# Second MLP layer as seven products of quarters, with the sums of the weight's quarters streamed from DRAM

## The chip, the cores and the metric

The kernel runs on one core of one Trainium2 chip. The metric is the device time of one execution in microseconds, the median of three runs. Instructions go to five engines, each with its own queue in program order: PE (matmul), DVE, ACT and POOL (elementwise work) and SP, which here only issues DMA transfers.

## The reference

Attention that keeps the 32 largest scores of each row, then a block with a Fourier mix and a two-layer MLP. All is float32; q, k and v are (8 batches, 8 heads, 576 tokens, 64), the weights 512x2048 and 2048x512.

```python
scores = q @ k.T / sqrt(64)
kth = np.partition(scores, -32, axis=-1)[..., -32:-31]
attn = softmax(np.where(scores >= kth, scores, -1e9))
x = (attn @ v)                       # heads joined: (8, 576, 512)
u = x + np.real(np.fft.fft(np.fft.fft(x, axis=1), axis=2))
un = (u - mean(u)) / np.sqrt(var(u) + 1e-6)     # over the 512 channels
out = u + np.maximum(un @ w_ch1, 0.0) @ w_ch2
```

## The kernel before

One loop counts steps `i`. A step is one 128-token tile of one head (or the 64 left-over tokens of two heads), 9 steps for a pair of heads, 36 for a batch (`PER_BATCH`), 288 for all (`N`). In a step PE computes scores for three steps ahead (`scores`) and ACT copies them from PSUM; DVE finds the 32 largest values by alternating MAX8 and MATCH_REPLACE8 (`top_ops`); ACT and POOL make the mask (`mask`), ACT the exponential (`expo`), and PE transposes the result two steps later (`transposes`) and multiplies it with v (`attend`).

Beside it goes the rest of a batch that has its attention behind it. POOL folds x into sums and differences (`fold_ops`), PE makes the DFT over the tokens (`dft_tokens`, tiles `yp`) and over the channels (`dft_channels`, tiles `mp`), adds the result to x and transposes it (`channels_first`, tiles `tpu`). Then the batch's MLP arrives as a queue of units (`mlp_units`). The five token tiles of a batch are two chunks: tiles 0, 1 and the 64 left-over tokens (320 columns), and tiles 2 and 3 (256 columns). For each chunk there are 16 units `hidden`, each of which makes 128 of the 2048 inner values, transposed, in PSUM tile `hp` and lets ACT write their ReLU to the SBUF tile `hT`; then units `back`: for a full tile 8 units of 2 products of 128x128 weights (a piece of hT) with 512 columns of w2, accumulated in one PSUM tile `cp`. The left-over tokens take 4 units, in which two halves of the inner sum go into two halves of the array. When a `cp` is done, ACT multiplies it by the row's 1/sqrt(var), POOL adds it to x, and SP stores x. For tile 3 DVE does both (`finish`), for the left-over tokens ACT and DVE.

The order of each engine is written by hand: `at(step, where, fn)` puts work at a step, `level` spreads the queued units evenly over the steps until the next batch's units arrive, and `some` lets units run between the fixed pieces of PE's work. w1, w2 and the tables stay in SBUF. SBUF tiles are named by `tag`, and tiles with one tag share a place: `hT` has one place, `S` (scores) six.

PSUM has eight banks of 512 float32 a partition: two for scores, two for transposes, one for the attention's product, and three (`ps_m`) for all that the MLP and the DFT make, and for a few other tiles, taken in turn.

The last batch has no attention beside it: after step 288 only its DFT and MLP (and the end of batch 6's MLP) are left.

Of the kernel before, what the change touches and what calls it, by code (L numbers as in the profile page):

```python
# [9 lines left out]
F32 = mybir.dt.float32  # L10
# [54 lines left out]
def kernel(  # L65
# [41 lines left out]
    batp = ctx.enter_context(tc.tile_pool(name="batp", bufs=1))  # L107
    small = ctx.enter_context(tc.tile_pool(name="small", bufs=4))
    ps_s = ctx.enter_context(tc.tile_pool(name="ps_s", bufs=2, space=bass.MemoryType.PSUM))
    ps_t = ctx.enter_context(tc.tile_pool(name="ps_t", bufs=2, space=bass.MemoryType.PSUM))  # L110
    ps_o = ctx.enter_context(tc.tile_pool(name="ps_o", bufs=1, space=bass.MemoryType.PSUM))
    ps_m = ctx.enter_context(tc.tile_pool(name="ps_m", bufs=3, space=bass.MemoryType.PSUM))

    ident = const.tile([P, P], F32, name="ident", tag="ident")
# [35 lines left out]
    def weight_steps(chunks, space, wc, slots):  # L150

        scaled = {}

        def words(n):
            o = 2 * wc * (n % slots)
            raw = space[:, o:o + 2 * wc]
            return raw, raw[:, 0:2 * wc:2], raw[:, 1:2 * wc:2]

        def load(n):
            if n < len(chunks):  # L160
                dst, src = chunks[n]
                if moe_w_ch1.dtype == F32:
                    nc.sync.dma_start(out=dst, in_=src)
                else:
                    nc.sync.dma_start(out=words(n)[0].bitcast(I32), in_=src.bitcast(I32))

        def scale_high(n):
            if moe_w_ch1.dtype == F32:
                return
            scaled[n] = ps_m.tile([P, wc], F32, name=f"wh_{n}", tag="mm")  # L170
            nc.scalar.activation(
                out=scaled[n], in_=words(n)[2], func=AF.Copy, scale=2.0 ** -112
            )

        def shift(n):
            if moe_w_ch1.dtype == F32:
                return
            nc.vector.tensor_scalar(
                out=chunks[n][0].bitcast(I32), in0=scaled.pop(n).bitcast(I32),
                scalar1=3, scalar2=None, op0=ALU.logical_shift_left,  # L180
            )

        def rest(n):
            if moe_w_ch1.dtype == F32:
                return
            _, low, high = words(n)
            nc.scalar.activation(
                out=low.bitcast(I32), in_=low.bitcast(U32), func=AF.Copy, scale=2.0 ** -29
            )
            nc.scalar.activation(out=high, in_=high.bitcast(I32), func=AF.Sign)  # L190

        def join(n):
            if moe_w_ch1.dtype == F32:
                return
            dst, (_, low, high) = chunks[n][0], words(n)
            bits = dst.bitcast(I32)
            nc.gpsimd.tensor_tensor(out=bits, in0=bits, in1=low.bitcast(I32), op=ALU.add)  # L197
            nc.gpsimd.tensor_tensor(out=dst, in0=dst, in1=high, op=ALU.mult)  # L198

        return load, scale_high, shift, rest, join  # L200


# [83 lines left out]
    def scores(i, part):  # L286
# [22 lines left out]
        if part == 1:  # L309

            pool, tag = (ps_s, "sp") if i else (ps_m, "mm")
            copy = nc.scalar.copy if i else nc.vector.tensor_copy
            sp = pool.tile([P, NF * P], F32, name=f"sp_{i}_t", tag=tag)

            q_end = P * t + rows
            nc.tensor.matmul(  # L316
                sp[:, 0:P], lhsT=qT[:, q_end - P:q_end], rhs=kt_t, start=True, stop=True
            )
            for h, (s_t, r, _, tails) in enumerate(to):
                copy(out=s_t[r, tails], in_=sp[P - rows:P, TAIL * h:TAIL * (h + 1)])  # L320
            return 0.3
# [156 lines left out]
    def to_tokens(pair, ch, at_once=True):  # L478
# [5 lines left out]
        xT, rd = xT_of.pop((pair, ch)), rd_of.pop((pair, ch))  # L484
        pool, tag = (ps_o, "o") if at_once else (ps_m, "mm")
        tp = pool.tile([P, 4, P], F32, name=f"tpx_{pair}_{ch}", tag=tag)
        for n, t in enumerate(CHUNKS[ch]):
# [104 lines left out]

    def dft_tokens(b, par):

# [3 lines left out]
        if b not in y_of:  # L598
            y_of[b] = batp.tile([P, 4, S], F32, name=f"y_{b}", tag="y")
        y = y_of[b]  # L600
        yps = [
            ps_m.tile([P, 2, KQ], F32, name=f"yp_{b}_{par}_{g2}", tag="mm") for g2 in range(2)
        ]

        def mm(g2, gg, st, lhsT, rows, table, start=False):

            nc.tensor.matmul(  # L607
                yps[g2][0:rows, gg, :],
                lhsT=lhsT,
# [6 lines left out]

        for g2 in range(2):
            for gg in range(2):
                g = 2 * g2 + gg
                for st in range(3):  # L620
                    f = fg[:, st] if st < 2 else ftail
                    mm(g2, gg, st, f[:, P * g:P * (g + 1)], P, gg, start=gg == 0 and st == 0)
        for st in range(3):
            mm(0, 1, st, zw[:, st, Q1:Q1 + 1] if st < 2 else ftail[:, DM:DM + 1], 1, 0)

# [3 lines left out]
        )  # L629
        for g2, yp in enumerate(yps):  # L630
            y2 = y[:, 2 * g2:2 * g2 + 2, :]
            nc.scalar.copy(out=y2[:, :, par:HS + 1:2], in_=yp[:, :, 0:KQ - par])
            nc.scalar.copy(out=y2[:, 0, mir], in_=yp[:, 0, back])
            nc.scalar.mul(out=y2[:, 1, mir], in_=yp[:, 1, back], mul=sg[:, g2:g2 + 1])
        if par == 1:
            tails_of_y(b)
        return 4.3

# [5 lines left out]
    def dft_channels(b, t, quick=False):  # L644

        rows, y = ROWS[t], y_of[b]
        mp = ps_m.tile([P, 2, DM // 2], F32, name=f"mp_{b}_{t}", tag="mm")
        for par in range(2):
# [61 lines left out]
    def channels_first(b, t):  # L710
# [3 lines left out]
        if (b, ch) not in unT_of:  # L714
            unT_of[b, ch] = batp.tile(
                [P, NDT, CW[0]], F32, name=f"unT_{b}_{ch}", tag="fold_s" if ch == 0 else "y"
            )
        tp = ps_m.tile([P, NDT, P], F32, name=f"tpu_{b}_{t}", tag="mm")
        for dt in range(NDT):
# [3 lines left out]
        nc.scalar.copy(out=unT_of[b, ch][:, :, col:col + rows], in_=tp[:, :, 0:rows])  # L723
        return 0.6

    def mlp_units(b):
# [4 lines left out]
        def hidden(ch, it):  # L733
            w, unT = CW[ch], unT_of[b, ch]
            if ch not in hTs:
# [3 lines left out]
                )  # L739
            hp = ps_m.tile([P, CW[0]], F32, name=f"hp_{b}_{ch}_{it}", tag="mm")  # L740
            for dt in range(NDT):
# [5 lines left out]

        cps, cts = {}, []

# [9 lines left out]
        def back(ch, t, part):  # L759
            n, hT, rs = CHUNKS[ch].index(t), hT_of[ch], rs_of[b]  # L760
            if part == 0:
                cps[t] = ps_m.tile([P, DM], F32, name=f"cp_{b}_{t}", tag="mm")
            cp = cps[t]
# [44 lines left out]
            if part == 3:  # L808
                ct = ct_of(t)
                for h in range(2):  # L810
                    r0 = TAIL + TH * h
                    nc.scalar.copy(out=ct[TH * h:TH * (h + 1), :], in_=cp[r0:r0 + TH, :])

                def finish():
                    xt, c = x[0:TAIL, 4, :], ct[0:TAIL]
                    nc.vector.tensor_tensor(out=c, in0=cp[0:TAIL], in1=c, op=ALU.add)
                    nc.vector.scalar_tensor_tensor(
                        out=xt, in0=c, scalar=rs[0:TAIL, 4:5], in1=xt, op0=ALU.mult, op1=ALU.add
                    )
                    for h in range(2):  # L820
                        tok = HS * h + 2 * P
                        nc.sync.dma_start(
                            out=out[b, tok:tok + TH, :], in_=x[TH * h:TH * (h + 1), 4, :]
                        )

                if last:
                    finish()
                else:
                    late_next.append(finish)

        units = []
        for ch in range(2):
            units += [
                (8 * CW[ch] / 1200.0, lambda ch=ch, it=it: hidden(ch, it), "hidden")
                for it in range(NIT)
            ]
            for t in CHUNKS[ch]:
                units += [
                    (1.75, lambda ch=ch, t=t, p=p: back(ch, t, p), "back")
                    for p in range(4 if t == 4 else 8)  # L840
                ]
        return units

# [97 lines left out]
    for c in range(DF // DM):  # L941
# [5 lines left out]
        )  # L947

    for b in range(B):
        end = PER_BATCH * (b + 1) - 1  # L950
# [39 lines left out]
        for par in range(2):  # L990
            at(ft[par], "pe1", lambda b=b, par=par: dft_tokens(b, par), 4.3)
        for n, t in enumerate((0, 1, 4, 2, 3)):
# [7 lines left out]
            if first and t == 4:  # L1000
                at(s + 1, "pe", lambda: (queue.extend(held), held.clear()) and 0.0)
        at(s + 1, "begin" if quick else "dve", lambda b=b: rsqrt(b))
        arrivals.append(s + (1 if quick else 2))
        at(arrivals[-1], "units", lambda b=b: (queue if b else held).extend(mlp_units(b)))

    queue, held, pending, written, now, out_next = [], [], [], set(), [0], []
    step_us = 6.0
# [13 lines left out]
    def level(i):  # L1021

        steps = range(i, next((a for a in arrivals if a > i), i + PER_BATCH))
        rest, lev = sum(u[0] for u in queue + held), 0.0
        while lev < 6.4 and sum(max(0.0, lev - fixed_cost(s)) for s in steps) < rest:
# [168 lines left out]
```

## Time and profile before

| | |
|---|---|
| median of three runs | 1944.0 us (1943.31 to 1945.73) |
| span of the profiled run | 1942.8 us |
| PE busy | 1831.8 us (94%) |
| DVE busy | 1577.0 us (81%) |
| ACT busy | 1205.3 us (62%) |
| POOL busy | 773.3 us (40%) |
| granted clock of PE, mean | 0.972 |
| DMA | 57.80 MB, mean 30 GB/s |

A busy share is a mean over the whole span. The page also divides the span into 40 slices, and there one sees which engine is full when. A group of instructions has a line, an engine, what it writes and reads, a count, its busy time and the mean length of one; the idle time after the bar is that of the engine just before them, with what ended it. PEld is PE's weight load.

### The profile page before, as it was taken

How to read it: one execution, taken by the hardware profiler on the slowest of the kernel's cores; microseconds unless marked ns; L12 is line 12 of the kernel's file. 1: busy time of each engine (PE TensorE's matmuls, PEld its weight loads, DVE VectorE, ACT ScalarE, POOL GpSimd, SP SyncE). 2: the span in 40 equal slices, each digit the busy share in tenths (PEclk: the TensorE clock that was granted, in tenths of full speed). 3: DMA queues.
4: the chain of work that ended last, by engine and by line, in shares of the span. 5: the costliest groups of instructions: out<-in, count | busy, mean ns of one | idle time of the engine just before them, and what ended most of it. 6: DMA issues, size and time to landing. Idle time of an engine off the chain costs nothing.

```text
span 1942.8 us, 27224 instructions
## 1 busy us (share of the span) xinstructions
PE 1831.8 (94%) x8624; PEld 1123.4 (58%) x8624; DVE 1577.0 (81%) x3245; ACT 1205.3 (62%) x3060; POOL 773.3 (40%) x1054
## 2 busy tenths in 40 slices
PE   6567799999999999999999999999999999998999
PEld 3344465564665656556664756556664756566655
DVE  8999989999999999888888879988888879843000
ACT  6878657776876667666666667666666757541100
POOL 4768642326523454235423444235523444222000
PEclk8877899999999999999999999999999999999999
DMA  5333000101001010010100110010000100000000
GB/s 164 105 90 106 19 13 19 33 19 30 19 19 33 19 30 13 13 33 19 30 19 19 27 24 21 11 33 19 24 19 24 27 24 19 1 14 1 11 14 11
DMA packets 133583, 57.80 MB, mean 30 GB/s; under 512 B 124352, under 2 KB 124480, under 8 KB 133440
## 3 DMA queue, kind: packets, MB, share of 16 engines
q1 hardware_dynamic: 132656, 55.85, 10.8%
q8 instruction: 69, 1.13, 0.2%
q14 instruction: 74, 0.61, 0.1%
q10 hardware_dynamic: 784, 0.21, 0.0%
HBM read 46.57 MB, written 9.44 MB: 29 GB/s over the span
## 4 chain that ended last, share of the span: by engine, by line
PE 79%; DVE 7%; POOL 7%; ACT 4%; issue 3%; DMA 0%; SPq 0%; POOLq 0%; DVEq 0%; ACTq 0%
PE hp L742 24%; PE cp L766 22%; PE o L448 7%; PE tpP L411 6%; PE sp L346 6%; PE yp L607 3%; DVE m L367 3%; PE cp L802 3%; DVE wk L369 2%; PE mp L656 2%; POOL wk L384 2%; PE sp_t L316 2%; POOL w L198 1%; POOL w L197 1%; PE tpk L260 1%
## 5 line engine op out<-in xcount | busy, mean ns | idle before, releaser
L384 POOL TENSOR_TENSOR wk<-S,wk 128x576 f32<-128x576 f32 x288 | 407.2, 1414 | 907.8 <-ACT wk L383 854.6
L367 DVE MAX8 m<-wk 128x8 f32<-128x576 f32 x864 | 623.7, 750 | 5.5
L742 PE MATMUL hp<-unT,w 128*128 128x256 f32 (+1 forms) x2048 | 539.0, 410 | 3.1 <-ACT unT L723 2.1
L766 PE MATMUL cp<-w,hT 128*128 128x512 f32 x1024 | 477.2, 598 | 0.0
L742 PEld LDWEIGHTS hp<-unT,w 128*128 128x128 f32 x2048 | 373.5, 191 | 126.2 <-issue 31.4
L369 DVE MATCH_REPLACE8 wk<-m,wk 128x576 f32<-128x576 f32 x576 | 427.7, 743 | 0.0
L766 PEld LDWEIGHTS cp<-w,hT 128*128 128x128 f32 x1024 | 179.4, 190 | 180.5 <-issue 179.9
L390 ACT ACTIVATE wk<-wk,nt 128x576 f32<-128x576 f32 x288 | 225.6, 783 | 54.3 <-POOL wk L384 53.4
L411 PE MATMUL tpP<-ident,wk 128*128 128x128 f32 x1152 | 185.4, 285 | 65.6 <-ACT wk L390 42.0
L414 ACT COPY PT<-tpP 128x512 f32<-128x512 f32 (+1 forms) x320 | 171.8, 549 | 119.1 <-PE tpP L411 116.5
L383 ACT ACTIVATE wk<-S,nt 128x576 f32<-128x576 f32 x288 | 227.7, 791 | 27.9 <-POOL nt L376 26.5
L411 PEld LDWEIGHTS tpP<-ident,wk 128*128 128x128 f32 x1152 | 140.9, 145 | 162.9 <-ACT wk L390 60.9
L746 ACT ACTIVATE hT<-hp 128x320 f32<-128x320 f32 (+1 forms) x256 | 105.1, 411 | 193.3 <-PE hp L742 191.0
L367 DVE MAX8 m<-S 128x8 f32<-128x576 f32 x288 | 214.0, 743 | 12.2 <-ACT S L320 11.9
L369 DVE MATCH_REPLACE8 wk<-m,S 128x576 f32<-128x576 f32 x288 | 213.8, 742 | 0.0
L448 PE MATMUL o<-PT,v 128*64 128x256 f32 (+3 forms) x1440 | 196.0, 416 | 2.1 <-ACT PT L414 1.6
L349 ACT COPY S<-sp 128x512 f32<-128x512 f32 (+1 forms) x264 | 142.2, 590 | 65.9 <-PE sp L346 65.6
L346 PE MATMUL sp<-kT,qT 64*128 64x512 f32 (+1 forms) x528 | 162.1, 675 | 4.3 <-ACT means L934 3.3
L448 PEld LDWEIGHTS o<-PT,v 128*64 128x64 f32 x1440 | 111.7, 153 | 75.7 <-issue 17.5
L780 DVE SCALAR_TENSOR_TENSOR x<-cp,gi,x 128x512 f32<-128x512 f32 x11 | 8.2, 746 | 128.3 <-PE cp L766 128.3
L316 PEld LDWEIGHTS sp_t<-kt,qT 128*128 128x128 f32 x320 | 56.4, 197 | 53.8 <-issue 20.0
L346 PEld LDWEIGHTS sp<-kT,qT 64*128 64x128 f32 (+1 forms) x528 | 43.0, 193 | 62.8 <-issue 44.5
(126 smaller groups left out, 1822.6 us busy)
## 6 DMA issues: line engine op xcount, KB each, us to landing
space<-in_moe_w_ch_dram SPq DMA_DIRECT2D x32, 512.0 KB, 3.6
nat<-in_q_dram SPq DMA_DIRECT2D x128, 64.0 KB, 2.1
v<-in_v_dram SPq DMA_DIRECT2D x128, 64.0 KB, 2.1
out_dram<-x SPq DMA_DIRECT2D x32, 256.0 KB, 2.1
nat<-in_k_dram SPq DMA_DIRECT2D x124, 64.0 KB, 2.1
nat<-in_q_dram SPq DMA_DIRECT2D x128, 8.0 KB, 1.7
v<-in_v_dram SPq DMA_DIRECT2D x128, 8.0 KB, 1.7
nat<-in_k_dram SPq DMA_DIRECT2D x124, 8.0 KB, 1.7
```

Of the source, the lines that this page charges most:

```text
L346: nc.tensor.matmul(sp[r], lhsT=qT[hd, q_cols], rhs=kT[hd, :], start=True, stop=True)
L349: nc.scalar.copy(out=s_t[r, keys], in_=sp[r])
L367: ops.append(lambda src=src, m8=m8: nc.vector.max(out=m8, in_=src))
L369: ops.append(lambda src=src, m8=m8: nc.vector.match_replace(w, m8, src, NEG))
L383: nc.scalar.activation(out=w, in_=Ssb[i], func=AF.Relu, scale=-FAR, bias=Nt[i][:, 1:2])
L384: nc.gpsimd.tensor_tensor(out=w, in0=Ssb.pop(i), in1=w, op=ALU.subtract)
L390: nc.scalar.activation(out=w, in_=w, func=AF.Exp, bias=Nt.pop(i)[:, 0:1], accum_out=den_t[pair % 3][:, c:c + 1],)
L411: nc.tensor.transpose(tp[:, c, :], p_sb[:, k0 + P * c:k0 + P * (c + 1)], ident)
L414: nc.scalar.copy(out=pt[:, NF * he:NF * (he + 1), col:col + w], in_=tp[:, :, o:o + w])
L448: nc.tensor.matmul(o[D * e:D * (e + 1), c0:c1], lhsT=vv[:, c, e, :], rhs=pt[:, 2 * NF if c == NF else NF * e + c, c0:c1], start=(c == 0), ...
L742: nc.tensor.matmul(hp[:, 0:w], lhsT=w1[:, dt, P * it:P * (it + 1)], rhs=unT[:, dt, 0:w], start=(dt == 0), stop=(dt == NDT - 1),)
L766: nc.tensor.matmul(cp, lhsT=hT[:, it, P * n:P * (n + 1)], rhs=w2[:, it, :], start=(it == 0), stop=(it == NIT - 1),)
```

## The change

A chunk's two full tiles times w2 is a product of a 2x2 block matrix (two token tiles, two halves of the inner 2048) with a 2x2 block matrix (two halves of the inner 2048, two halves of the 512 columns). The ordinary way needs eight products of quarters. Winograd's form of Strassen's scheme needs seven, with sums of quarters on both sides:

```text
S1 = A21 + A22   S2 = S1 - A11   S3 = A22 - S2   S4 = A12 - S2
T1 = B12 - B11   T2 = B22 - T1   T3 = B22 - B12  T4 = B21 - T2
P1 = A11 B11  P2 = A12 B21  P3 = S4 B22  P4 = A22 T4
P5 = S1 T1    P6 = S2 T2    P7 = S3 T3
U2 = P1 + P6   U3 = U2 + P7
C11 = P1 + P2   C12 = P5 + P3 + U2   C21 = P4 + U3   C22 = P5 + U3
```

Its purpose is to give PE an eighth less to multiply in the second layer. Batch 0 stays as it was. For batches 1 to 7:

- POOL makes T1 to T4 once, during batch 1's attention (`parts_of_w2`, 4 subtractions for each of 8 pieces), and SP writes them with B21 to a tensor in DRAM (`scr`, five parts of 8 pieces of 128x256).
- The places of w2's quarters B12 and B21 in SBUF (16 pieces) become a ring. `stream` lists the pieces in the order of their use; `take` hands the next one to a product, and once that is issued its place is refilled from DRAM by SP (`refill`), which waits for the product. B11 and B22 stay. After the last attention step six tiles of tag `S` add 12 places (`more_places`).
- POOL makes S1 to S4 in place in hT (`mix`, one operation on 8 pieces of 128x128 each).
- A product has 8 matmuls of 128x128 weights with 256 columns, in two units of four. P1, P2, P5 and P3 go through the two halves of PSUM tile X (`cx`), P4, P6 and P7 through Y (`cy`); the order is P1, P4, P2, P5, P6, P7, P3.
- ACT multiplies a result and POOL adds it to x, in pieces of 256 columns (`summed`); DVE makes U2 and U3 (`both`), and ACT and POOL bring them to x (`spread`). In the last batch DVE does all of it.
- X and Y live long, so the three banks of `ps_m` are now handed out by `bank`, which skips those that are held. `dft_tokens` is cut into two calls for each parity, with one tile each.
- The left-over tokens use B11 and B22, and then T1 and B21 from the stream (`tails`), with 256 columns a matmul.

The core of the diff:

```diff
+    def bank(shape, name, hold=False):
+        while turn[0] in held:
+            turn[0] = (turn[0] + 1) % 3
+        n = turn[0]
+        turn[0] = (n + 1) % 3
+        t = ps_m.tile(shape, F32, name=name, tag=f"m{n}", bufs=1)
...
-        yps = [
-            ps_m.tile([P, 2, KQ], F32, name=f"yp_{b}_{par}_{g2}", tag="mm") for g2 in range(2)
-        ]
+        yp = bank([P, 2, KQ], f"yp_{b}_{par}_{g2}")
...
+    for _ in range(B - 1):
+        for ch in range(2):
+            stream += [(o, kc) for o in (T4, B21, T1, T2, T3) for kc in range(NK)]
+            if ch == 0:
+                stream += [(o, kc) for kc in range(NK) for o in (T1, B21)]
...
+    def refill():
+        while places and coming:
+            n, (o, kc) = coming.pop(0)
+            loaded[n] = places.pop(0)
+            nc.sync.dma_start(out=loaded[n], in_=scr[:, o, kc, :])
...
+            def product(dst, a, of, part, start=False):
+                for kc in range(NK // 2 * part, NK // 2 * (part + 1)):
+                    rhs, done = of(kc)
+                    nc.tensor.matmul(
+                        dst, lhsT=h()[a][:, kc, :], rhs=rhs, start=start and kc == 0,
+                        stop=kc == NK - 1, skip_group_check=True,
+                    )
+                    done()
...
+            def mix(dst, a, c, op=ALU.subtract):
+                v = h()
+                nc.gpsimd.tensor_tensor(out=v[dst], in0=v[a], in1=v[c], op=op)
...
+            def p2(part):
+                product(got["X"][:, 0, :], "12", streamed(B21), part)
+                if part:
+                    summed(ta, lo, got["X"][:, 0, :], 3)
+                    mix("12", "12", "11")
+
+            def p5(part):
+                product(got["X"][:, 1, :], "21", streamed(T1), part)
+                if part:
+                    summed(tb, hi, got["X"][:, 1, :], 2)
...
+            units = [
+                (1.75, lambda f=f, part=part: f(part), "back")
+                for f in (p1, p4, p2, p5, p6, p7, p3) for part in range(2)
+            ]
...
+            if b:
+                units += fast(ch)
+                continue
...
+    for kc in range(NK):
+        at(PER_BATCH + 14 + 2 * kc, "pool", lambda kc=kc: parts_of_w2(kc))
+    at(PER_BATCH + 14, "load2", lambda: nc.sync.dma_start(out=scr[:, B21], in_=w2[:, NK:, 0:DH]))
+
+    at(N + 4, "load", more_places)
...
         for par in range(2):
-            at(ft[par], "pe1", lambda b=b, par=par: dft_tokens(b, par), 4.3)
+            for g2 in range(2):
+                at(ft[par], "pe1", lambda b=b, par=par, g2=g2: dft_tokens(b, par, g2), 2.15)
```

## The prediction

> **What bounds the kernel now.** I read the page's busy slices first, then the groups kept apart by shape, the timeline of PE, the windows and the waits. The slices say where an engine is full:
>
> ```profile
> PE   6567799999999999999999999999999999998999
> DVE  8999989999999999888888879988888879843000
> PEclk8877899999999999999999999999999999999999
> ```
>
> A slice is 48.6 us. DVE fills the first five (batch 0's attention, PE half idle). From slice 6 on PE is full to the end, at the full clock; after slice 36 there is no attention left and only PE works. The second layer of batches 1 to 7 lies from about 510 us on, all inside PE's full stretch. Between 800 and 1700 us the view of waits for PE lists five entries, 4.8 us in all. So there, time taken off PE's own work is time off the end, and a new wait of PE is time on it. What the concerned groups cost:
>
> ```profile
> L766 PE MATMUL cp<-w,hT 128*128 128x512 f32 x1024 | 477.2, 598 | 0.0
> L742 PE MATMUL hp<-unT,w 128*128 128x256 f32 x1024 | 240.3, 382 | 0.0
> L802 PE MATMUL cp<-w,hT 128*64 128x512 f32 x256 | 61.1, 603 | 0.0
> ```
>
> L766 has 8 x 64 = 512 products but 1024 records: each f32 product is two records. The mean is a latency; matmuls overlap, so the price is the spacing of starts in a long run:
>
> ```profile
> 1716.68 3.65 PE L802 MATMUL cp<-w,hT 128*64 128x512 f32 x16
> 1720.27 0.66 PE L411 MATMUL tpP<-ident,wk 128*128 128x128 f32 x4
> ...
> 1735.46 7.07 PE L742 MATMUL hp<-unT,w 128*128 128x256 f32 x32
> 1742.37 0.60 PE L411 MATMUL tpP<-ident,wk 128*128 128x128 f32 x4
> ...
> 1749.92 2.38 PE L448 MATMUL o<-PT,v 128*64 128x256 f32 x20
> 1752.23 3.72 PE L742 MATMUL hp<-unT,w 128*128 128x256 f32 x16
> ...
> 1802.37 12.18 PE L766 MATMUL cp<-w,hT 128*128 128x512 f32 x28
> 1814.39 16.05 PE L742 MATMUL hp<-unT,w 128*128 128x320 f32 x59
> ```
>
> First column start, second length. 28 records of 512 columns take 12.02 us: 429 ns each. 32 of 256 columns (a new weight load for each) take 6.91 us: 216 ns. So the price is proportional to columns, and halving the columns exposes no weight load. 64-row products of 512 columns: 3.59/16 = 224 ns; of 256 columns: 2.31/20 = 116 ns.
>
> **What the skill says.** (1) "TensorE: Matmul & The Clock Gate", Step-by-step: the next weights load while the present matmul streams. The trace agrees: loads are recorded at 190 ns, and 216 ns spacing holds. (2) "PSUM — Partial Sum Buffer", PSUM bank collisions: two engines may not touch one bank at a time, even at different columns, so order is kept by bank. Before, a tile has a bank to itself in this pool and nothing shows this; after, two products share a held bank. (3) "DMA: Bandwidth & Descriptors", Latency: some 2 us of fixed cost for a transfer. The DMA part of the page agrees, 2.1 us for 64 KB and 256 KB. (4) "GPSIMD Engine Reference", Specifications: SBUF interfaces shared with VectorE, with contention only for some DVE forms. MAX8 has 743 and 750 ns means whatever POOL does, so I charge nothing.
>
> **The change part by part.**
>
> Removed, for each of seven batches: 64 products of 512 columns, 64 x 2 x 0.429 = 54.9 us of PE. Added: 2 chunks x 7 products x 8 = 112 of 256 columns, 112 x 2 x 0.216 = 48.4. Saved 6.5 us a batch, 45.8 in all. The 64-token tail goes from 32 records of 224 ns to 64 of 116: +0.2 a batch, +1.5 in all. Net PE work: −44.3 us.
>
> The stream: 96 blocks of 128 KB a batch, 672 in all, refilled as a product has consumed its place. 16 places are four units of PE (1.7 us each) ahead, and units share PE with attention, so a refill has about 10 us; 28 places after attention. A transfer takes about 2.1 us to land. The queue's price of an issue is 0.48 us:
>
> ```profile
> 14.80 1.92 SPq L214 DMA_DIRECT2D nat<-in_q_dram  x4
> ```
>
> so 46 us more SP time per batch of some 215, where it now has about 50. A refill waits on SP for PE, and behind it stand the loads of q, k and v, needed four steps (24 us) later: free. In batch 7 PE eats a block in 0.43 us and SP refills in 0.48, but 28 are in hand for 40: free. DMA is under a tenth busy now. A wait on a landed transfer costs PE nothing visible: the five transposes of k with DMA waits at 826.82 us go in 0.54 us, as fast each as tpP's four in 0.43.
>
> POOL gains, per batch, 8 sums of 128x1024 (2.36 us, row L580), 8 adds of 256 columns (about 0.72, L549's 256-column row), two of 1.27 and two of 0.72, less three of 1.27: +25 us, from 87 to 112 of 215. Behind each stands the mask (L384) of the next tile, but
>
> ```profile
> POOL wk L384 <- ACT wk L383: 483.8, 128, 8.7
> ```
>
> says that in 800 to 1700 us POOL stood 484 us waiting for ACT before it, 3.8 us a time; a sum of 2.4 us goes there. ACT +4 us and DVE +1.2 us a batch are beside PE's work too. The 32 subtractions that make w2's sums (23 us of POOL, steps 50 to 64) lie in a POOL that is 30% busy; I charge 1 us.
>
> New waits of PE, from the instruction orders of both programs:
>
> (a) Two of the three banks of this pool are held by a chunk's X and Y. For batches 2 to 6 one pair of DFT tiles (yp) then shares the one bank that is left, with no unit between, so PE waits for ACT's three copies:
>
> ```profile
> 939.72 0.43 ACT L632 COPY y<-yp 128x288 f32<-128x288 f32 x1 [4.28 <-PE yp L607]
> 940.03 0.29 ACT L633 COPY y<-yp 128x144 f32<-128x144 f32 x1
> 940.20 0.41 ACT L634 ACTIVATE y<-yp,sg 128x144 f32<-128x144 f32 x1
> 940.47 0.43 ACT L632 COPY y<-yp 128x288 f32<-128x288 f32 x1
> ```
>
> 0.75 us, plus a drain of 0.16 (0.41 long, 0.25 spacing) and 0.2 of hand-over: 1.1 x 5 = 5.5 us.
>
> (b) In batches 3, 5 and 6 mp_0 and mp_1 share a bank too. Here ACT is late:
>
> ```profile
> 941.37 3.72 PE L656 MATMUL mp<-fd,y 128*128 128x256 f32 x16
> 944.74 1.17 ACT L673 COPY us<-mp 128x512 f32<-128x512 f32 x2
> ```
>
> mp_0's eight records end at 943.2, its copy at 945.3, as exp, score copies and a mask lie before it on ACT: 2.2 us x 3 = 6.6.
>
> (c) p5 writes the bank that ACT reads for p2 (the skill's point 2). Mostly other work of PE or a free ACT hides it; three chunks have only 0.43 us of transposes between, three of the last two batches nothing: 3 x 0.3 + 3 x 0.65 = 2.8.
>
> (d) Before batch 7's layer all fourteen tiles go through one bank, where ACT or DVE (0.6 to 0.7 us, plus 0.2) must empty each; units stand between some. About 0.4 + 4 x 0.85 + 3 x 0.75 = 6.0. Before, the same place has waits of 0.96 and 0.35, left as they are.
>
> (e) Batch 1's layer lies at 510 to 740 us, where DVE is nearly full as well:
>
> ```profile
> 631.41:680.00 48.59, 48.59 (x251) 33.53 (x250) 46.17 (x96) 33.89 (x88) 23.86 (x35) 1.00 0.09 19
> 825.69:874.30 48.61, 48.61 (x243) 28.19 (x242) 41.12 (x84) 31.30 (x80) 17.26 (x27) 1.00 0.13 33
> ```
>
> (Columns: PE, PE's loads, DVE, ACT, POOL.) At 631 DVE is 95% busy, at 826 85%. I count half of that batch's 6.5: −3.3 of gain.
>
> Sum: −44.3 + 5.5 + 6.6 + 2.8 + 6.0 + 3.3 + 1.0 = −19.1: **1925 us**. The doubtful prices are (a) to (d), 20.9 us: none if ACT is prompt and PE's waits displace others (1904), twice that if ACT is later than in the trace (1946).
>
> **The rivals.**
>
> Clean gain: the waits a to d mostly vanish, because a PE that has less work waits where it would have waited anyway, or ACT is prompt. For it: PE is the only full engine after 780 us. Against it: PE's order is fixed and these pairs stand back to back. 1925 less 20.9: about 1904 us.
>
> DVE or the chain over POOL takes over: DVE is needed 190 us of a batch's 215, in some stretches 95%; POOL's sums wait for PE in order, and mask, exp and transposes come behind. If half of the gain of batches 1 to 6 goes so (39 us x 1/2, less e) on top of the waits: 1925 + 16 = 1941. Against it: POOL's 3.8 us of slack and exp's place, 6 us after the mask.
>
> The stream starves PE, the side of slower: SP works strictly in order; stores that wait for POOL or DVE and blocks of 8 loads (8 x 0.48 = 3.8 us) stand between refills. If each of 14 chunks lost 3.8 us: 1925 + 53 = 1978. Against it: four units of lead.
>
> **How the numbers follow.** Forecast 0.52, clean 0.22, DVE or POOL 0.16, starved 0.10. The range 1902 to 1942 leaves out the starved case and the ends of the others. Faster: forecast, clean, and two thirds of the third case, 0.84; same (1940 to 1948) 0.05; slower: the starved case and the worst of the rest, 0.11.
>
> **What would show it.** Right: products of 256 columns at 216 ns spacing, no DMA among PE's waits, PE waits at yp, mp and tpu released by ACT or DVE of about 20 us, POOL near 960 us busy. Wrong: spacing above 230 ns in the streamed products (then weights or waits are exposed), DMA waits of PE, tpP waiting for exp, or DVE above 95% in every batch.

## The result

The changed kernel is slower: 1968.07 us (1964.51 to 1970.73, four runs) against 1944.76 us for the kernel before (four runs of its own). The ratio is 1.0119, with a 95% interval of 1.0098 to 1.0141. The profiled run has a span of 1964.0 us, 21.2 more than before.

### The profile page after: what moved, and what is told of

Read it like the earlier page. It is cut to its first block, busy times and chain, and to the rows that moved or that the text cites. A ratio compares the mean times of both kernels' runs of the same rounds, so it can differ in the third digit from the quotient of the medians.

```text
span 1964.0 us, 30502 instructions
## 1 busy us (share of the span) xinstructions
PE 1806.4 (92%) x9520; PEld 1275.7 (65%) x9520; DVE 1591.4 (81%) x3284; ACT 1225.0 (62%) x3128; POOL 961.6 (49%) x1196
## 4 chain that ended last, share of the span: by engine, by line
PE 69%; POOL 15%; ACT 6%; issue 5%; DVE 5%; DMA 0%; SPq 0%; POOLq 0%; DVEq 0%; ACTq 0%
PE hp L820 23%; PE cx L941 7%; PE o L465 7%; PE cy L941 6%; PE sp L363 5%; PE tpP L428 5%; POOL wk L401 4%; PE yp L622 3%; PE cp L1064 3%; PE mp L670 3%; POOL hT L960 2%; PE cp L844 2%; DVE m L384 2%; POOL w L215 2%; POOL w L214 2%
## 5 line engine op out<-in xcount | busy, mean ns | idle before, releaser
L401 POOL TENSOR_TENSOR wk<-S,wk 128x576 f32<-128x576 f32 x288 | 408.2, 1417 | 753.4 <-ACT wk L400 725.3
L400 ACT ACTIVATE wk<-S,nt 128x576 f32<-128x576 f32 x288 | 226.8, 788 | 94.4 <-POOL nt L393 93.4
L407 ACT ACTIVATE wk<-wk,nt 128x576 f32<-128x576 f32 x288 | 224.6, 780 | 75.6 <-POOL wk L401 74.2
L941 PE MATMUL cx<-w,hT 128*128 128x256 f32 x848 | 205.0, 388 | 10.0 <-issue 10.0
L941 PEld LDWEIGHTS cx<-w,hT 128*128 128x128 f32 x848 | 157.8, 194 | 39.7 <-issue 20.4
L960 POOL TENSOR_TENSOR hT<-hT 128x1024 f32<-128x1024 f32 x56 | 132.3, 2363 | 102.6 <-ACT hT L824 95.4
L941 PE MATMUL cy<-w,hT 128*128 128x256 f32 x648 | 156.2, 387 | 0.0
L941 PEld LDWEIGHTS cy<-w,hT 128*128 128x128 f32 x648 | 120.1, 193 | 24.6 <-issue 8.9
```

The lines of the kernel that those rows point to most:

```text
L400: nc.scalar.activation(out=w, in_=Ssb[i], func=AF.Relu, scale=-FAR, bias=Nt[i][:, 1:2])
L401: nc.gpsimd.tensor_tensor(out=w, in0=Ssb.pop(i), in1=w, op=ALU.subtract)
L407: nc.scalar.activation(out=w, in_=w, func=AF.Exp, bias=Nt.pop(i)[:, 0:1], accum_out=den_t[pair % 3][:, c:c + 1],)
L941: nc.tensor.matmul(dst, lhsT=h()[a][:, kc, :], rhs=rhs, start=start and kc == 0, stop=kc == NK - 1, skip_group_check=True,)
L960: nc.gpsimd.tensor_tensor(out=v[dst], in0=v[a], in1=v[c], op=op)
```

## The profile after

The page first: the totals, the slices that were shown of before and, as the last line, the chain that ended last, by engine:

```profile
PE 1806.4 (92%) x9520; PEld 1275.7 (65%) x9520; DVE 1591.4 (81%) x3284; ACT 1225.0 (62%) x3128; POOL 961.6 (49%) x1196
PE   6666799998999999999999999999999999998899
DVE  8999989998999979987888969897889878852110
PEclk8777899999999999999999999999999999999999
PE 69%; POOL 15%; ACT 6%; issue 5%; DVE 5%; DMA 0%; SPq 0%; POOLq 0%; DVEq 0%; ACTq 0%
```

The slices still look full, since a digit 9 hides up to a tenth. The sums tell more: PE is busy 25.4 us less than before, not 44, and idle 157.6 us (1964.0 − 1806.4) against 111.0. In the chain POOL has 15%, where it had 7% before:

```profile
PE 79%; DVE 7%; POOL 7%; ACT 4%; issue 3%; DMA 0%; SPq 0%; POOLq 0%; DVEq 0%; ACTq 0%
```

A window over most of the second layer shows the same. Columns: stretch, its length, then busy time (and instructions) of PE, PE's loads, DVE, ACT and POOL, the granted clock, DMA share and GB/s. Before:

```profile
480.00:1760.00 1280.00, 1268.70 (x6159) 780.55 (x6155) 1109.01 (x2293) 837.35 (x2136) 512.59 (x735) 1.00 0.09 21
```

After:

```profile
480.00:1760.00 1280.00, 1229.48 (x6762) 887.33 (x6759) 1110.33 (x2309) 847.65 (x2179) 638.05 (x814) 0.99 0.28 78
```

PE was idle 11.3 us of 1280, and is now idle 50.5. What it waits for is scattered, so I looked for the wait inside the attention loop that had grown most. It is one of ACT: in the view of waits over the whole run (time, number, longest) ACT's mask activation (L383 before, L400 after) waits for the bounds `nt` that POOL makes from the tile's largest and 32nd largest value. Before, then after:

```profile
ACT wk L383 <- POOL nt L376: 26.5, 21, 3.8
ACT wk L400 <- POOL nt L393: 93.4, 52, 4.9
```

One place in full, from the chain of waits (start, length, what; `issue` is time for which the profile shows no releaser):

```profile
915.98 0.73 POOL x L956
916.71 2.33 POOL hT L960
919.04 2.47 POOL zw L566 x2
921.51 0.16 POOL nt L393
921.67 0.02 issue
921.70 0.78 ACT wk L400
922.48 0.07 issue
922.55 1.41 POOL wk L401
923.96 1.35 issue
925.30 5.09 PE cx L941 x16
```

POOL works without a gap from 915.98: an addition to x, a sum of hidden blocks (L960), two folds of the DFT, and only then the bounds, which take 0.16 us. ACT stands at L400 until then, and behind it in ACT's queue are the exponential (L407), which also waits for POOL's subtraction L401, and the scaling (L955) that reads P2's result out of PSUM tile X. P5 goes into the other half of the same bank, so PE goes on with `cx` only when ACT has read it. ACT's and PE's timelines (start, length, what, and in brackets the idle time before; the last line is a place where PE has not waited):

```profile
921.70 0.77 ACT L400 ACTIVATE wk<-S,nt 128x576 f32<-128x576 f32 x1 [3.81 <-POOL nt L393]
923.98 0.78 ACT L407 ACTIVATE wk<-wk,nt 128x576 f32<-128x576 f32 x1 [1.04 <-POOL wk L401]
924.75 0.45 ACT L955 ACTIVATE hT<-cx,gi 128x256 f32<-128x256 f32 x1
921.61 0.49 PE L333 MATMUL sp_t<-kt,qT 128*128 128x128 f32 x2
925.30 5.09 PE L941 MATMUL cx<-w,hT 128*128 128x256 f32 x16 [3.21 <-issue]
711.85 3.62 PE L941 MATMUL cy<-w,hT 128*128 128x256 f32 x16
```

The reader is to see two losses: 3.21 us of waiting, and 16 records that take 5.09 us instead of 3.62. PE's granted clock is recorded as half for 3.41 us from 924.72 us on. The trace's clock records have seven such stretches between 500 and 1760 us; the trace of before has none there.

## The experiments

In all of them the kernel before was run beside the others on the same chip, 1942 to 1946 us. Ratios are to it, with their 95% interval. "Sums" are POOL's eight operations L960 a batch. The expectations call PE TensorE, DVE VectorE, ACT ScalarE and POOL GpSimd.

**Are the sums the cause?** The sums are left out (`mix` returns at once), so the output isn't the layer's.

```diff
             def mix(dst, a, c, op=ALU.subtract):
-                v = h()
-                nc.gpsimd.tensor_tensor(out=v[dst], in0=v[a], in1=v[c], op=op)
+                return
```

> After with the eight sums of hidden blocks per batch (L960, 56 of 2.36 us) left out, so the products multiply the plain blocks and the output is not the layer's; products, stream, banks, scaling and adds stay. Theory A (GpSimd's sums stand in its queue before the bounds of the next tile, L393; ScalarE's mask activation L400 waits for those, its copies out of PSUM come behind, TensorE waits and then runs at half clock): the loss goes, 1925 us (1915 to 1935), and ScalarE's wait at L400 falls from 93 us to about the 27 of before. Rival B (shared and held PSUM banks), rival C (stream) and rival D (256-column products cost more than their share): no change, 1962 to 1970.

Measured: 1929.42 us, 0.9927 (0.9912 to 0.9942). The sums cost 38.7 us, more than the whole loss. The rest of the change gains 14.8 us, not far from the 19 forecast. PE's busy time:

```profile
PE 1785.5 (93%) x9520; PEld 1264.4 (66%) x9520; DVE 1588.3 (82%) x3284; ACT 1225.7 (64%) x3128; POOL 830.9 (43%) x1140
```

The saving of PE is 46.3 us (1831.8 − 1785.5). The spans of the two profiled runs differ by 35.8 us, and the loss lies beside attention: its last transposes start at 1769.4 us with the sums and at 1734.6 without. Ahead of the changed layer, up to 480 us, PE is busy 4.8 us longer with the sums, which costs nothing, since the stretch is as long in both. From 480 us on, PE is busy 16.1 us longer for the same work and idle 19.7 us longer. The idle time is nearly all in three waits up to the end of attention: at `cx` 9.4 us (no wait shown there without the sums), at the transposes `tpP` for the exponential 10.3 (3.8), at `yp` for ACT's copies 8.6 (5.0). L400's wait fell from 93 to 42 us, where 27 was expected.

**By which way do they cost?** First the sums were put behind the bounds of their step:

```diff
-                nc.gpsimd.tensor_tensor(out=v[dst], in0=v[a], in1=v[c], op=op)
+                todo.append(lambda: nc.gpsimd.tensor_tensor(
+                    out=v[dst], in0=v[a], in1=v[c], op=op
+                ))
...
+                    at(now[0], "pool", flush)
```

> After with the same sums put into GpSimd's queue behind the bounds of their step instead of ahead of them. Theory A: the wait at L400 shrinks, but the sums now stand ahead of the next mask's subtraction L401, on which the exponent and the transposes wait: 1930 to 1950. If only GpSimd's sum of busy time counted: 1968. Rivals B, C, D: 1968.

Measured: 1955.04 us, 1.0051 (1.0034 to 1.0068), a little outside the expected range. A third of what the sums cost goes. L400 waits 23 us instead of 72 between 500 and 1700 us, but now L407, the exponential, waits 74 us for POOL's subtraction L401 instead of 51. POOL stands twice in each tile's chain, and the sums are now ahead of the other place.

Then the bounds were moved from POOL to VectorE (`nc.gpsimd` to `nc.vector` in `bounds`), in the changed kernel and in the one before.

> After with the bounds (L393, 128x2) computed by VectorE right behind the last maximum instead of by GpSimd. Theory A: ScalarE's L400 never waits for GpSimd, only the subtraction L401 is queued behind the sums: 1925 to 1945. Rival, the whole chain over GpSimd is late and not just the bounds: 1955 to 1968, the wait moves from L400 to L407. Rivals B, C, D: 1968, or a little slower by VectorE's 288 more instructions.

> Before with the same move of the bounds to VectorE. Theory A: ScalarE's wait there was only 26.5 us in 21 places and TensorE hardly idled, so a gain of 3 to 8 us: about 1939. If bounds over GpSimd cost something everywhere, more than 15 us. If VectorE is the closer bound: slower by up to 20.

Measured: 1969.43 us, 1.0131 (1.0116 to 1.0146), and 1949.89 us, 1.0029 (1.0017 to 1.0040). Both expectations of theory A are missed. The test had a second effect, which the expectations named only as rivals: in batch 1's layer VectorE has no room. Windows of the changed kernel:

```profile
600.00:700.00 100.00, 95.17 (x557) 70.28 (x555) 94.70 (x194) 65.68 (x176) 54.03 (x64) 0.98 0.28 78
700.00:800.00 100.00, 95.70 (x505) 66.86 (x504) 90.69 (x194) 70.76 (x183) 46.26 (x70) 0.98 0.19 54
```

and of the kernel with the bounds on VectorE (third number: DVE):

```profile
600.00:700.00 100.00, 95.86 (x563) 70.49 (x562) 98.90 (x211) 68.64 (x182) 47.14 (x46) 0.98 0.29 81
700.00:800.00 100.00, 92.25 (x497) 64.78 (x497) 98.85 (x207) 68.14 (x174) 46.31 (x54) 0.97 0.23 64
```

So it looks as if a wait was traded for a full engine, and the run says little on the bounds. The clean form puts them on ScalarE, which has room:

```diff
-            nc.gpsimd.tensor_tensor(
-                out=Nt[i], in0=M8.pop(i)[:, 0:TOPK:TOPK - 1], in1=cc, op=ALU.mult
-            )
...
+        nc.scalar.mul(out=Nt[i][:, 1:2], in_=m[:, TOPK - 1:TOPK], mul=FAR)
+        nc.scalar.mul(out=Nt[i][:, 0:1], in_=m[:, 0:1], mul=-1.0)
         nc.scalar.activation(out=w, in_=Ssb[i], func=AF.Relu, scale=-FAR, bias=Nt[i][:, 1:2])
```

> After with the bounds computed by ScalarE itself, two 128x1 multiplications right ahead of the mask's activation, so neither GpSimd nor more of VectorE's time is in the way of L400 (the move to VectorE made that engine the bound, 98.9% busy in batch 1). If the wait for the bounds is what costs: 1930 to 1945. If the subtraction L401 behind the sums costs as much, or ScalarE's extra 0.4 us a tile: 1960 to 1975.

> Before with the bounds on ScalarE. Theory A2: GpSimd had 26.5 us of L400's kind of wait here and the chain gets 0.2 us shorter, ScalarE gets 0.4 us a tile more: 1940 to 1946. If the move is worth in itself what it was worth in e8 (20 us), 1925: then the change's own loss is not what e8 repaired.

Measured: 1947.27 us, 1.0016 (1.0009 to 1.0023), 20.8 us less than the changed kernel; and 1940.99 us, 0.9987 (0.9980 to 0.9993) in the kernel before, where the same move brings 2.7. With the bounds on ScalarE the sums cost 19.0 us (against 1928.28 us without them, below) instead of 38.7. So about half of what the sums cost went through the bounds.

**A wait inside the sums, or their time?** The page says that the sums themselves stood 95 us waiting for ScalarE's last ReLU. To see if that is the harm, each sum was issued one step later, right behind the subtraction of the mask (`at(now[0] + 1, "act", flush)`); and, in another kernel, replaced at its place by two additions of zeros on a 64x464 part that waits for no ReLU (1.92 us the pair, and the output isn't the layer's). The same idle additions were put into the kernel before.

```diff
-                v = h()
-                nc.gpsimd.tensor_tensor(out=v[dst], in0=v[a], in1=v[c], op=op)
+                for _ in range(2):
+                    d = ftail[TAIL:P, 0:464]
+                    nc.gpsimd.tensor_tensor(out=d, in0=d, in1=d, op=ALU.add)
```

> After with each sum issued in the next step, right behind the subtraction of that step's mask, instead of in the middle of its own step (same sums, same layer). Theory A1 (what hurts is that a sum stands at the head of GpSimd's queue waiting for ScalarE's last Relu, 95 us in 14 batches' halves, with the mask's chain behind it): that wait is gone, so 1929 to 1938 us, near the run without the sums. Theory A2 (the sums' own 2.36 us each, 132 us in all, wherever they stand in the chain, are what delays the mask): 1950 to 1965.

> After with each sum replaced, at the same place, by two idle additions on 64x464 (about 2.4 us together) that touch no block of the hidden layer and so wait for no ScalarE; the products multiply plain blocks and the output is not the layer's. Theory A1 (the wait for ScalarE's Relu in GpSimd's queue): 1929 to 1938. Theory A2 (the time on GpSimd itself): 1955 to 1968.

> Before with the same idle additions, eight times a batch in batches 1 to 7, at the units where the change has its sums. Theory A2 (GpSimd's time ahead of the bounds is what costs): clearly slower, 1965 to 1985. Theory A1 (waits, not time): 1944 to 1952.

Measured: 1965.25 us, 1.0107 (1.0092 to 1.0122); 1967.40 us, 1.0119 (1.0104 to 1.0134); and 1954.92 us, 1.0053 (1.0038 to 1.0068). Idle work costs as much as the real sums, so it is POOL's time at this place, and theory A1 falls. Its premise was a misreading, which the view of waits would have shown:

```profile
POOL hT L960 <- ACT hT L824: 95.4, 3, 47.7
```

These are three waits, all behind the last attention step, where no mask stands behind them. In the next step the sums wait there just as long, so that run did not take the wait away; and inside attention it has the next tile's bounds behind the sums again. The idle sums also cost as much although a pair takes 1.92 us, not the 2.4 expected. But the kernel before lost only 10.8 us by nearly the same load, which neither theory expected.

**Where can the sums stand?** With the bounds on ScalarE: each sum in the next step behind the subtraction; the same with at most one sum a step and none in a step with folds; the same with at most one sum a step, fold steps included; the second chunk's sums of batches 2 to 7 on VectorE; and no sums at all, as the floor (whose output isn't the layer's).

> Bounds on ScalarE as in e8, and each sum issued one step later, right behind the subtraction of the mask, as in e5. Theory A2 (GpSimd's time between VectorE's maximum and TensorE's transposes is what costs; the sums are harmless only in the gap after the subtraction, once the bounds no longer stand behind them there): 1930 to 1940. If the place does not matter once the bounds are away: 1947 as e8.

> As e9, but at most one sum a step, none in a step with GpSimd's folds unless a product needs it. Theory A2 (lumps on GpSimd, one behind another, hold the subtraction L401): a little better than e9, 1927 to 1938. If only the sum of GpSimd's time counts: as e9.

> As e9 (bounds on ScalarE, sums behind the next step's subtraction), but at most one sum a step, fold steps included. If two sums beside a fold in one step make e9's remaining loss: 1932 to 1940. If not: 1943 to 1948; if products come to wait for late sums: more, as e11.

> As e9, but the second chunk's four sums of batches 2 to 7, which meet GpSimd's folds, on VectorE (about 12% idle there). If GpSimd's time beside the folds is what is left: 1930 to 1940. If VectorE has no room either: 1945 to 1960.

> e8 with the sums of hidden blocks left out (the output is not the layer's): the floor for any placing of the sums. Theory A2: e1's 1929 less a few us for the bounds: 1922 to 1930. If ScalarE's 0.4 us a tile costs by itself: 1930 to 1940.

| | us | ratio to before (95%) |
|---|---|---|
| sums in the next step | 1945.10 | 1.0002 (0.9993 to 1.0010) |
| spread, none beside folds | 2030.06 | 1.0441 (1.0424 to 1.0459) |
| at most one a step | 1932.19 | 0.9942 (0.9927 to 0.9957) |
| a part on VectorE | 1931.35 | 0.9937 (0.9922 to 0.9952) |
| no sums | 1928.28 | 0.9918 (0.9904 to 0.9933) |

The first is near what was expected if the place does not matter, the second misses both of its expectations, and the other three lie in the better of the ranges given. The first left a place like this one in its chain of waits, at the fold steps:

```profile
899.17 1.42 POOL wk L400
900.59 2.33 POOL hT L963
902.92 0.07 issue
902.99 2.16 POOL hT L963
905.14 0.17 issue
905.31 0.74 POOL x L955
906.05 2.46 POOL zw L565 x2
908.51 1.37 POOL wk L400
909.88 1.35 issue
911.23 3.69 PE cx L940 x16
```

Two sums, an addition and two folds stand between two tiles' subtractions (L400 here), 9.3 us apart. With one sum a step the chain over the same place is PE's own, and what is left of the wait is 0.67 us:

```profile
903.85 2.31 PE o L464 x20
906.16 0.42 PE sp_t L333 x2
906.58 0.67 issue
907.25 3.69 PE cx L940 x16
```

Spreading too far is worse than any of it: sums that wait for a step without folds come too late for their products, and PE waits for them.

```profile
PE cy L940 <- POOL hT L972: 37.6, 10, 5.8
PE cx L940 <- POOL hT L972: 35.3, 7, 5.9
```

The versions with one sum a step and with VectorE's part compute the whole layer, beat both kernels and are within 4 us of the floor. About 3 us of the gain is the bounds' move, which the kernel before would have too (1940.99 us).

**Why so much here and so little before?** Two attempts. First, half of PE's product work was left out of the changed kernel (`if kc % 2:` ahead of the matmul in `product`; the output isn't the layer's), with and without the sums.

> After with every second matmul of the seven products left out (392 of 784 of 0.216 us, 85 us of TensorE's work; the output is not the layer's), the sums on GpSimd kept. Theory R (the loop with the sums is the bound in the attention part): only the tail's share of about 12 us and little more comes off, 1935 to 1955. Theory S (sums add idle time to TensorE's work): 85 us less, about 1883.

> The same without the sums. Theory R: clearly faster than e13, by more than the 39 us that the sums cost in the whole kernel, 1860 to 1895. Theory S: faster than e13 by 39 us, about 1845.

Measured: 1898.89 us, 0.9775 (0.9760 to 0.9789), and 1846.58 us, 0.9506 (0.9490 to 0.9522). Theory R as written (a loop that sets the time whatever PE does) is wrong: 69 us came off with the sums kept. Nor is theory S right: the sums now cost 52 us. The expectations also priced the work left out at half of what it is: a matmul is two records, so 784 records of 0.216 us, 169 us, are gone, and without the sums PE is busy 142 us less (1785.5 − 1643.1). Only 83 us of that came off the end and PE stands idle 57 us more, so its work is no longer all that sets the time there, and that 1846.58 lies near the expected 1845 is luck. Second, the plain second layer in all batches, but with the changed kernel's holding of PSUM banks, with and without idle sums.

```diff
             if part == 0 and b and t != 4:
+                if t in (0, 2):
+                    spare.append(turn[0])
+                    held.add(turn[0])
+                cps[t], frees[t] = bank([P, DM], f"cp_{b}_{t}", True)
```

> The plain second layer of before in all batches (no Strassen products, no stream, no parts of w2), in the changed kernel's arrangement of PSUM: the product's bank and one more of the three are held through each pair of tiles, so one is left for all else; the idle sums of e6 and e7 on GpSimd. Theory H: the sums cost as much here as in the changed kernel, 35 us or more over e18, so 1985 or above. Theory R in part: 10 to 15 us over e18, about 1958 to 1965.

> The same without the idle sums: what holding the banks costs by itself. By the prediction's terms for shared banks (5.5, 6.6 and 6.0 us): up to 18 us over before, 1946 to 1962. If held banks cost nothing without late engines: 1943 to 1946.

Measured: 1996.53 us, 1.0271 (1.0250 to 1.0293), and 1978.68 us, 1.0180 (1.0163 to 1.0197). Theory H is not borne out: the idle sums cost 18 us here. But the banks alone cost 35 us, above the range that I gave. PE's waits between 500 and 1700 us without the sums:

```profile
PE mp L670 <- ACT us L687: 12.4, 8, 1.7
PE yp L622 <- ACT y L648: 6.1, 6, 1.0
PE tpu L734 <- ACT us L687: 3.2, 4, 0.8
PE tpu L734 <- ACT unT L737: 2.9, 4, 0.7
```

So the sums cost 11 us on the plain kernel, 18 with its banks held, 39 in the changed kernel and 52 with half of its products. The profiled runs, from 480 us on, part this:

| | plain | banks held | changed | half products |
|---|---|---|---|---|
| span longer by, us | 7.5 | 18.4 | 35.8 | 53.3 |
| PE busy longer, same work | 1 | 7 | 16 | 18 |
| PE idle longer | 6 | 11 | 20 | 35 |
| half clock recorded longer, up to the end of attention | 0 | 14 | 20 | 38 |

Half of the last row comes near the second, so the longer work is, for the most part, the clock. The idle time is what differs. ACT's wait for the bounds, from 480 us to the end of attention, grows by 41 us on the plain kernel (9.9 to 51.0), by 36 with its banks held and by 55 in the changed kernel; so ACT comes late in all three, and what differs more is how much of it reaches PE. The changed kernel has one thing that the plain one with held banks lacks: two products in one bank, and 9.4 of its 20 us are waits at `cx`. Its POOL also has more other work (830.9 us without the sums, 773.3 in the kernel before). No run separates these, and half products are a different case again, with more idle time to begin with: that stays open.

## Why the prediction was wrong

- **PE's work.** Forecast −44.3 us net. Without the sums PE is busy 46.3 us less, 42.4 of it from 480 us on, so this holds. (The tail's term is 7 × 0.256 = 1.8 us rather than 1.5, which changes nothing.)
- **Waits at shared banks and the rest of the costs.** Forecast 25.2 us, 3.3 of it a gain that batch 1 doesn't get. Without the sums PE's idle time grows by 31.7 us (142.7 − 111.0), 27.8 of it from 480 us on, and the run took 1929.4 us where 1925 was forecast. Singly, between 500 and 1700 us of that run: `yp` 5.0 us in 5 waits (5.5 forecast), `mp` 4.3 in 3 (6.6). These terms were right to within a few us. That the sum comes out too is partly luck: `o` waits 6.1 us in three places for DVE, which no term had. For the plain layer with held banks the terms would have been too small by half, so the agreement belongs to this arrangement. (c), the wait of P5 for ACT at P2, was priced at 2.8 us; without the sums it is 1.8, all in the last batch; with them `cx` waits 9.4 us up to the end of attention alone.
- **The stream.** PE's products wait for no transfer of it and their weight loads for 1.8 us in all; 624 blocks landed in 2.6 us, the median (2.1 assumed). The rival in which the stream starves PE is false.
- **POOL: the step that failed.** Its busy time was forecast at 960 and is 961.6 us, and it was charged nothing: "a sum of 2.4 us goes there", into 3.8 us of waiting a time before the subtraction. That term measured 38.7 us. The 3.8 us was a mean over 128 waits, taken in front of one of POOL's two operations on each tile. In the steps with folds there was no such slack, as the place at 916 us shows. Between the subtractions of two tiles the sums stand at 34 places of the trace; 15 of these hold folds too, and 10 hold two sums. And the wait used was POOL's own. What counts is who waits for POOL: ACT, with its copies out of PSUM behind it, and then PE. A sign that the prediction gave for being wrong did come: `tpP` waits for the exponential, 10.3 us in 11 places between 500 and 1700 us.
- **The rival that held.** The case with the chain over POOL named the mechanism ("POOL's sums wait for PE in order, and mask, exp and transposes come behind") but gave 1941 us and a chance of 0.16. It charged half of a gain of 39 us, while the sums took 38.7. Its wording was also off: idle sums that wait for neither PE nor ReLU cost the same.
- **The clock.** No term stood for it. PE has idled so little before that its clock never fell between 500 and 1760 us; "PE's waits displace others" has an opposite, waits that make the work after them slower. Of the 35.8 us between the profiled runs, 16.1 are work that ran longer, and the clock is at most 10 of these: an estimate from seven stretches of 3.41 us at half clock, against one without the sums (at 486 us).
- **DVE.** The charge of nothing for POOL's extra load was right, though not by the lines it rests on: 743 and 750 ns are MAX8's means on two input tiles, not under two loads of POOL. With POOL 49% busy they are 743 and 751.

## What to carry to other kernels

Work that is put on an engine with half its time free must be checked step by step against what stands behind it in that engine's queue, and against who waits for that; a mean wait in front of one instruction is not slack in every step. Put such work behind the engine's last due instruction of a step, one piece a step, but not later than its user needs it: here that, together with the bounds' move to ScalarE, turned a loss of 1.2% into a gain of 0.6%. The place alone did nothing as long as the bounds stood behind it (1965 us). And before moving an operation to relieve a wait, look at the fullest engine by stage: the same move brought nothing on VectorE (1969 us against 1968) and 20.8 us on ScalarE.

## What was not expected of the hardware

- **Half clock after short waits.** The Trainium skill, "TensorE: Matmul & The Clock Gate", What's actually happening, gives the half-rate state after an idle window of about 3.4 us. The trace agrees in the length: each of the seven stretches is recorded with 3.41 us. But PE had not been idle for all of the 3.41 us before them: 1.1 to 3.2 us, as far as the records show, 2.6 before the stretch at 924.72 us and 2.3 before that at 1235.33. They give no threshold, since the 3.41 us from 1010.05 us on, with 1.8 us idle, are followed by none. The seven start at 685.79, 702.85, 924.72, 1153.41, 1235.33, 1375.28 and 1593.73 us, which are 5, 65, 67, 24, 41 and 64 times 3.413 us apart, so it seems to count how idle PE was within a fixed stretch, not how long one wait is; no run tests this. The price: after a wait of 3.21 us 16 records took 5.09 us instead of 3.62, and after one of 2.42 us 20 records of `o` took 4.58 instead of 2.91:

```profile
1234.25 4.58 PE L465 MATMUL o<-PT,v 128*64 128x320 f32 x20 [2.42 <-DVE x L509]
957.26 2.91 PE L465 MATMUL o<-PT,v 128*64 128x320 f32 x20
```

- **A sum on VectorE.** The skill's "GPSIMD Engine Reference", Key points, has VectorE about twice as fast in elementwise work. Here the same 128x1024 sum took 1469 ns on VectorE and 2364 ns on POOL, 1.6 times.
